# Stage heads of a fused attention and feed-forward kernel: other PSUM banks for the plain tiles, a centring read from PSUM, and another order of the first weight sums

## The chip, the cores and the metric

The kernel runs on one core of one Trainium2 chip. The metric is the device time of one execution in microseconds, taken as the median of several runs. TensorE (PE) multiplies matrices, with PEld for its weight loads; VectorE (DVE), ScalarE (ACT) and GpSimd (POOL) work element by element; SyncE (SP) issues transfers. Each engine takes its instructions in the order in which they were written, and waits for others by semaphores.

## The reference

```python
# q, k, v: (8, 12, 448, 64) float32;  g_ln: (768,);  w_ch1: (768, 3072);  w_ch2: (3072, 768)
scores = matmul(q, k.transpose(0, 1, 3, 2)) / sqrt(64)
attn_out = matmul(maximum(scores, 0.0) ** 2 / 448, v)
x = attn_out.transpose(0, 2, 1, 3).reshape(8, 448, 768)
mu = mean(x, axis=-1);  var = mean((x - mu) ** 2, axis=-1)
xn = (x - mu) / sqrt(var + 1e-06) * g_ln
out = x + maximum(xn @ w_ch1, 0.0) @ w_ch2
```

The division by the root of the variance is one factor per row. Since it is positive it passes through the ReLU, and the kernel multiplies by it at the very end.

## The kernel before, in words

**Stages.** The eight batches go in four pairs. Attention of batches 0 and 1 comes first, interleaved with their first feed-forward layer. Then, for pair 0, 1 and 2, the second layer of the pair (`ffn2`, 56 units of six matmuls: 7 tiles of tokens x 2 halves x 4 parts, L628) is interleaved with the attention of the next pair. Before the second layer of pairs 1 and 2, and of pair 3, stands the first layer of that pair. This place is called a stage head here. There are three: at about 174, 301 and 428 us of the profile.

**Order.** The program order is written out by hand; there is no scheduler that changes it. In `interleave` the attention units are all placed by the last but one of the 56 units, so a stage ends: product of the last attention group (`values`, L363), three units, `centre` of the odd batch, one last unit (L628), whose result DVE finishes with L639.

**Layout.** Activations lie transposed: the 768 channels are six chunks of 128 partitions, and the 448 tokens of a batch lie along the free dimension. `xT` is the attention output, `xc` the same times g_ln, later centred. `lo` and `hi` are the `xc` of the even and odd batch of a pair.

**Centring.** `centre` (L408) sums all channels by matmuls with a matrix of ones (L418) into `sum_ps`. ScalarE copies the sum into SBUF (`total_sb`, L422; only the very first block skips that), and six DVE instructions, one per chunk (L424), subtract the mean from `xc`. For whole batches GpSimd has summed the chunks in advance (L398, L401) and split the sum into two bf16 tiles, `two_sb` (L404, L405).

**PSUM.** There are eight banks. Two belong to `ps_mm` throughout. The other six are, in attention stages, three two-bank tiles of `ps_sc` (scores, products, `sum_ps`), and at the heads of pairs 1 to 3 six one-bank tiles of `ps_m`. A plain tile is one `ffn1` call: six matmuls (L590) into one `ps_mm` bank, then a ReLU on ScalarE (L598) into `hT`. `ffn2` uses `ps_mm` too.

**Heads of pairs 1 and 2.** `ffn1_pair` (L654) computes the first layer for both batches of a pair at once. Of the 24 blocks of hidden channels, four are plain tiles (`beside`: four of the even batch, then four of the odd one). The other twenty go in ten sets of two blocks; in a set the two batches, the two halves of the channels and the two blocks form a 2 x 2 by 2 x 2 product, done with seven block products in place of eight (Strassen). Each product is three matmuls of 448 columns (L715). It needs sums of activations (`x_sum`, and `x[6]` and `x[7]`, L740 and L741, which overwrite parts of `hi` and `lo`), made once a head, and sums of weight blocks, made for each set: two early ones for products 3 and 4 (L694, L695) and three late ones for products 6, 1 and 7 (L702, L706, L707). The order in a set is 3, 4, 1, then 7 and 6 of the set before (`close`), then 5 and 2. DVE adds the results up: L748 and L750 add products 4 and 1 to `z`; L757 and L760 form `z - a` and `z - b`, on which products 7 and 6 are accumulated. Early sums run two sets ahead on GpSimd, late sums one set ahead on DVE.

**Memory of the sums.** `w_room[0]` and `w_room[1]` are attention buffers; `w_room[2]` and the later `z` tiles lie in `room`, the buffer of `xT`, which is free once the transfer L562 has turned `xT` into token order. `temps[0]` and `temps[1]`, the `z` of sets 0 and 1, are the buffers with the tags "total" and "two".

**Head of pair 3.** Here all 24 tiles of each batch are plain tiles, 48 `ffn1` calls. DVE forms weight sums for the second layer meanwhile (L789).

Of the kernel before, what the change touches and what calls it, by code (L numbers as in the profile page):

```python
# [28 lines left out]
def kernel(  # L29
# [22 lines left out]
    nc = tc.nc  # L52
    P = 128
    HP = 64
    bf16 = mybir.dt.bfloat16
    fp32 = mybir.dt.float32

    B, H, S, D = q.shape
# [8 lines left out]
    K2 = d_ff // P  # L67
# [20 lines left out]
    spool = ctx.enter_context(tc.tile_pool(name="stat", bufs=2))  # L88
# [3 lines left out]
    ps_mm = ctx.enter_context(tc.tile_pool(name="ps_mm", bufs=2, space=bass.MemoryType.PSUM))  # L92
# [64 lines left out]
    for queue, name, lo, hi in ((nc.sync, "q", 0, FEW), (nc.scalar, "k", 0, FEW),  # L157
                                (nc.sync, "k", FEW, J), (nc.scalar, "q", FEW, J)):
        s = slice(lo * D, hi * D)
# [139 lines left out]
    FULL = (0, J)  # L299
    FIRST = (0, BLK[0][0])  # L300
# [106 lines left out]

    def centre(b, blk):  # L408
        w = blk[1] * HP
        if (b, blk) == FIRST:  # L410
            ps = ps_mm.tile([P, 512], fp32, tag="mm", name="sum_ps")[:, :w]
        else:
            ps = ps_sc.tile([P, 2, 512], fp32, tag="sc", name="sum_ps")[:, 0, :w]
        rows = [xT[b // 2][:, c, of(blk, b)] for c in range(K1)]
        if blk == FULL:
            rows = [part[b][:, i] for i in range(2)] + (rows[4:] if b % 2 else [])
        for i, r in enumerate(rows):
            nc.tensor.matmul(ps, ones, r, start=(i == 0), stop=(i == len(rows) - 1))  # L418
        total = ps
        if (b, blk) != FIRST:  # L420
            total = spool.tile([P, S], fp32, tag="total", name="total_sb", bufs=1)[:, :w]
            nc.scalar.copy(total, ps)  # L422
        for c in range(K1):
            nc.vector.scalar_tensor_tensor(  # L424
                xc[b][:, c, of(blk)], total, g_mean[:, c:c + 1], xc[b][:, c, of(blk)],
                op0=ALU.mult, op1=ALU.add)
# [152 lines left out]

    since = [9]  # L580

    def ffn1(b, ni, blk):


        pair, o, w = b // 2, b % 2 * S + blk[0] * HP, blk[1] * HP
        if pair not in hT:
            hT[pair] = hpool.tile([P, K2, S2], bf16, tag="hT", name="hT_sb")
        ps = ps_mm.tile([P, 512], fp32, tag="mm", name="h_ps")
        for c in range(K1):
            nc.tensor.matmul(  # L590
                ps[:, :w], w1[:, c, ni * P:(ni + 1) * P], xc[b][:, c, of(blk)],
                start=(c == 0), stop=(c == K1 - 1))
        since[0] += 1
        turns = 2 if (b, blk) == FIRST else 1
        if blk != FULL and since[0] <= turns:
            nc.vector.tensor_scalar_max(hT[pair][:, ni, o:o + w], ps[:, :w], 0.0)
        else:
            nc.scalar.activation(hT[pair][:, ni, o:o + w], ps[:, :w], ACTF.Relu)  # L598
        if since[0] >= turns:
            squares_now()  # L600
# [51 lines left out]
    KQ = K1 // 2  # L652

    def ffn1_pair(pair, rows, beside):  # L654

        lo, hi = xc[2 * pair], xc[2 * pair + 1]  # L660
        hold_x = [apool.tile([P, 2, 512], bf16, tag="attn", name="x_sum")[:, :, :S] for _ in range(5)]
        x = {3: lo[:, :KQ], 4: hi[:, KQ:], 6: hi[:, :KQ], 7: lo[:, KQ:]}
        for m, t, rest in ((5, 0, (3, 0)), (2, 1, (3, 1)), (1, 2, (4, 0))):
            x[m] = (hold_x[t][:, 0], hold_x[t][:, 1], hold_x[rest[0]][:, rest[1]])
        w_room = [[apool.tile([P, 2, 512], bf16, tag="attn", name="w1_sum").rearrange("p r n -> p (r n)")
                   for _ in range(2)] for _ in range(2)]
        temps = [spool.tile([P, S], fp32, tag="total", name="z_sb", bufs=1),
                 spool.tile([P, 2, S], bf16, tag="two", name="z_sb", bufs=1)
                 .rearrange("p i s -> p (i s)").bitcast(fp32)]
        room = xpool.tile([P, K1, S2], bf16, tag="xT", name="room_sb")  # L670
        rest = room[:, KQ:].rearrange("p c s -> p (c s)")
        w_room.append([rest[:, :1024], rest[:, 1024:2048]])
        temps += [room[:, n].bitcast(fp32) for n in range(KQ)]

        def x_sum(m, a, b):
            nc.vector.tensor_add(hold_x[{5: 0, 2: 1, 1: 2}[m]], a[:, :2], b[:, :2])
            (nc.gpsimd if m == 1 else nc.vector).tensor_add(x[m][2], a[:, 2], b[:, 2])

        x_sum(5, lo[:, :KQ], lo[:, KQ:])
        w = {}  # L680

        def blocks(n):
            i, j = rows[n]
            i, j = slice(i * P, (i + 1) * P), slice(j * P, (j + 1) * P)
            return w1[:, :KQ, i], w1[:, :KQ, j], w1[:, KQ:, i], w1[:, KQ:, j]

        def sums_early(n, engine):
            if n >= len(rows):
                return
            b11, b12, b21, b22 = blocks(n)  # L690
            one, two = (t.rearrange("p (c n) -> p c n", n=P) for t in w_room[n % 3])
            w[n] = {2: b11, 5: b22, 6: one[:, :3], 1: one[:, 3:6], 3: two[:, :3], 4: two[:, 3:6],
                    7: (one[:, 6], one[:, 7], two[:, 6]), "61": one[:, :6], "7a": one[:, 6:8]}
            engine.tensor_sub(w[n][3], b12, b22)  # L694
            engine.tensor_sub(w[n][4], b21, b11)  # L695

        def sums_late(n):
            if n >= len(rows):
                return
            b11, b12, b21, b22 = blocks(n)  # L700
            j = slice(rows[n][1] * P, (rows[n][1] + 1) * P)
            nc.vector.tensor_add(  # L702
                w[n]["61"].rearrange("p (h c) n -> p h c n", h=2),
                b11.unsqueeze(1).broadcast_to([P, 2, KQ, P]),
                w1[:, :, j].rearrange("p (h c) n -> p h c n", h=2))
            nc.vector.tensor_add(w[n]["7a"], b21[:, :2], b22[:, :2])  # L706
            nc.vector.tensor_add(w[n][7][2], b21[:, 2], b22[:, 2])  # L707

        def bank():
            return ps_m.tile([P, 512], fp32, tag="m", name="m_ps")[:, :S]  # L710

        def product(n, m, ps, first=True):
            for c in range(KQ):
                at = [a[c] if isinstance(a, (list, tuple)) else a[:, c] for a in (w[n][m], x[m])]
                nc.tensor.matmul(ps, *at, start=(first and c == 0), stop=(c == KQ - 1),  # L715
                                 skip_group_check=not first)

        def relu(n, ps, row, half):
            nc.scalar.activation(  # L719
                hT[pair][:, rows[n][row], half * S:(half + 1) * S], ps, ACTF.Relu)  # L720

        open_ = []

        def close():
            n, a, b = open_.pop()
            product(n, 7, a, False)
            relu(n, a, 0, 0)
            product(n, 6, b, False)
            relu(n, b, 1, 1)

        for unit in beside[:4]:
            unit()
        x_sum(2, hi[:, :KQ], hi[:, KQ:])
        x_sum(1, lo[:, :KQ], hi[:, KQ:])
        sums_early(0, nc.vector)
        sums_late(0)
        sums_early(1, nc.gpsimd)
        for unit in beside[4:]:
            unit()
        nc.vector.tensor_sub(x[7], lo[:, KQ:], hi[:, KQ:])  # L740
        nc.gpsimd.tensor_sub(x[6], hi[:, :KQ], lo[:, :KQ])  # L741
        for n in range(len(rows)):
            z = temps[n] if n < 2 else temps[2 + n % KQ]
            a, b, c = bank(), bank(), bank()
            product(n, 3, a)
            nc.scalar.copy(z, a)
            product(n, 4, b)
            nc.vector.tensor_add(z, z, b)  # L748
            product(n, 1, c)
            nc.vector.tensor_add(z, z, c)  # L750
            if open_:
                close()
            sums_early(n + 2, nc.gpsimd)
            sums_late(n + 1)
            product(n, 5, a, False)
            relu(n, a, 1, 0)
            nc.vector.tensor_sub(a, z, a)  # L757
            product(n, 2, b, False)
            relu(n, b, 0, 1)
            nc.vector.tensor_sub(b, z, b)  # L760
            open_.append((n, a, b))
        return close
# [125 lines left out]

    def ffn1_units(b, blk=FULL):
        if blk == FULL:  # L890
            return [lambda ni=ni: ffn1(b, ni, blk) for ni in range(K2)]
        return [lambda: ffn1_head(b, blk)] + [lambda ni=ni: ffn1(b, ni, blk) for ni in range(3, K2)]

    def ffn2_units(pair):
# [55 lines left out]
    for pair in range(pairs - 1):  # L950
        units = ffn2_units(pair)
        if pair:
            wide.close()
            ps_m = open_narrow()
            tokens(pair)
            first, second = ffn1_units(2 * pair), ffn1_units(2 * pair + 1)
# [18 lines left out]
    ps_m = open_narrow()  # L975
# [56 lines left out]
```

## Time and profile before

| | us |
|---|---|
| runs (median, lowest to highest) | 539.34 (539.16 to 539.63) |
| profiled execution, its own time | 540.06 |
| its span, first to last instruction | 538.3 |
| TensorE busy | 523.7 (97%) |
| DVE busy | 377.7 (70%) |
| ScalarE busy | 281.1 (52%) |
| GpSimd busy | 156.3 (29%) |

The profile shows one execution. A span begins with the first instruction; the execution's own time is 1.76 us longer. A line of the timeline gives start, duration, engine, line, operation, output and inputs, shape and count, and in brackets how long the engine had been idle and which instruction's end released it. Successive instructions of one engine may overlap by a little, so the pitch from start to start is less than the duration. Matmul ends are modelled. The granted TensorE clock is 1.00 of full speed in this profile.

### The profile page before, as it was taken

How to read it: one execution, taken by the hardware profiler on the slowest of the kernel's cores; microseconds unless marked ns; L12 is line 12 of the kernel's file. 1: busy time of each engine (PE TensorE's matmuls, PEld its weight loads, DVE VectorE, ACT ScalarE, POOL GpSimd, SP SyncE). 2: the span in 40 equal slices, each digit the busy share in tenths (PEclk: the TensorE clock that was granted, in tenths of full speed). 3: DMA queues.
4: the chain of work that ended last, by engine and by line, in shares of the span. 5: the costliest groups of instructions: out<-in, count | busy, mean ns of one | idle time of the engine just before them, and what ended most of it. 6: DMA issues, size and time to landing. Idle time of an engine off the chain costs nothing.

```text
span 538.3 us, 11408 instructions
## 1 busy us (share of the span) xinstructions
PE 523.7 (97%) x4666; PEld 309.8 (58%) x4666; DVE 377.7 (70%) x727; ACT 281.1 (52%) x472; POOL 156.3 (29%) x178
## 2 busy tenths in 40 slices
PE   8999999999999999999999989999999999999997
PEld 6677779755555445555555445555555545555665
DVE  5775753378887888767898788757889797024643
ACT  6956775456543366656555256745655244441110
POOL 7334102123425465002625474201230300001321
PEclk9999999999999999999999999999999999999999
DMA  9999999999997901118997950204741150000223
GB/s 198 206 206 207 211 180 179 142 165 155 161 163 135 195 2 13 22 30 137 169 172 149 168 85 2 34 16 84 126 93 44 32 117 1 0 1 2 58 60 88
DMA packets 111301, 56.64 MB, mean 105 GB/s; under 512 B 77330, under 2 KB 111250, under 8 KB 111250
## 3 DMA queue, kind: packets, MB, share of 16 engines
q0 software_dynamic: 26976, 25.50, 31.9%
q1 hardware_dynamic: 83490, 29.77, 30.3%
q8 instruction: 36, 0.59, 0.4%
q10 hardware_dynamic: 784, 0.66, 0.4%
q14 instruction: 15, 0.12, 0.1%
HBM read 51.91 MB, written 11.01 MB: 117 GB/s over the span
## 4 chain that ended last, share of the span: by engine, by line
PE 91%; DMA 2%; DVE 2%; ACT 2%; POOL 2%; issue 1%; DVEq 0%; ACTq 0%; POOLq 0%
PE o_ps L628 31%; PE h_ps L590 23%; PE m_ps L715 12%; PE m_ps L829 8%; PE sc_ps L333 7%; PE av_ps L363 6%; DMA w<-in_moe_w_ch_dram 2%; PE o_ps L884 1%; PE h_ps L612 1%; PE sum_ps L418 1%; ACT hT_sb L598 1%; ACT early L344 1%; PE tr_ps L218 1%; POOL v_sb L128 0%; POOL w L146 0%
## 5 line engine op out<-in xcount | busy, mean ns | idle before, releaser
L628 PE MATMUL o_ps<-w,hT_sb 128*128 128x384 bf16 x1008 | 173.4, 326 | 0.0
L344 ACT ACTIVATE attn_sb<-sc_ps 128x896 bf16<-128x896 f32 (+4 forms) x150 | 126.4, 902 | 82.1 <-PE sc_ps L333 69.3
L628 PEld LDWEIGHTS <-hT_sb 128*128 128x128 bf16 x1008 | 94.9, 98 | 75.0 <-issue 15.2
L590 PE MATMUL h_ps<-xc_sb,w 128*128 128x448 bf16 (+2 forms) x888 | 128.6, 300 | 4.5 <-ACT hT_sb L598 3.8
L590 PEld LDWEIGHTS <-w 128*128 128x128 bf16 x888 | 81.5, 98 | 47.7 <-issue 8.4
L346 DVE TENSOR_TENSOR attn_sb<-attn_sb 128x896 bf16<-128x896 bf16 x126 | 81.6, 662 | 31.6 <-ACT attn_sb L344 29.8
L598 ACT ACTIVATE hT_sb<-h_ps 128x448 bf16<-128x448 f32 (+2 forms) x133 | 59.5, 447 | 64.9 <-PE h_ps L590 64.3
L719 ACT ACTIVATE hT_sb<-m_ps 128x448 bf16<-128x448 f32 x80 | 43.4, 544 | 27.9 <-PE m_ps L715 26.6
L401 POOL TENSOR_TENSOR part_sb<-part_sb,xT_sb 128x448 f32<-128x448 f32 x18 | 23.3, 1295 | 55.1 <-DVE xT_sb L370 54.4
L715 PE MATMUL m_ps<-xc_sb,w_sum 128*128 128x448 bf16 x168 | 36.3, 352 | 2.8 <-DVE m_ps L757 2.8
L424 DVE SCALAR_TENSOR_TENSOR xc_sb<-total_sb,g_mean,xc_sb 128x448 bf16<-128x448 f32 (+2 forms) x54 | 29.0, 606 | 12.8 <-ACT total_sb L422 12.8
L398 POOL TENSOR_TENSOR part_sb<-xT_sb 128x448 f32<-128x448 bf16 x6 | 6.6, 1105 | 105.0 <-DVE xT_sb L370 83.0
L569 DVE BATCH_NORM_STATS2 stats<-xtok_sb 128x6 f32<-128x384 bf16 x56 | 28.0, 541 | 11.3 <-DMA xtok_sb<-xT_sb 11.3
L333 PE MATMUL sc_ps<-qT_sb,kT_sb 64*64 64x448 bf16 x504 | 35.0, 358 | 0.0
L639 DVE SCALAR_TENSOR_TENSOR o_sb<-o_ps,rstd_sb,xtok_sb 128x384 f32<-128x384 f32 (+1 forms) x45 | 26.9, 597 | 9.4 <-PE o_ps L884 5.6
L715 PEld LDWEIGHTS <-w_sum 128*128 128x128 bf16 x210 | 20.4, 98 | 22.5 <-issue 3.6
L370 DVE TENSOR_SCALAR xT_sb<-av_ps 128x896 bf16<-128x896 f32 (+2 forms) x30 | 27.0, 901 | 7.8 <-PE av_ps L363 7.7
L363 PE MATMUL av_ps<-attn_sb,v_sb 64*64 64x448 bf16 (+2 forms) x672 | 32.3, 327 | 0.0
L864 POOL TENSOR_TENSOR z_sb<-z_sb 128x384 f32<-128x384 f32 x3 | 4.2, 1385 | 91.5 <-DVE z_sb L863 82.1
L363 PEld LDWEIGHTS <-v_sb 64*64 64x64 bf16 x840 | 22.7, 107 | 11.8 <-issue 1.6
L386 DVE TENSOR_SCALAR xc_sb<-xT_sb,g_sb 128x448 bf16<-128x448 bf16 (+2 forms) x54 | 26.4, 539 | 1.0
L715 PE MATMUL m_ps<-x_sum,w 128*128 128x448 bf16 x120 | 26.0, 352 | 0.0
(124 smaller groups left out, 584.2 us busy)
## 6 DMA issues: line engine op xcount, KB each, us to landing
out_dram<-o_sb SPq DMA_DIRECT2D x85, 96.0 KB, 2.4
v_sb<-in_v_dram POOLq DMA_DIRECT2D x24, 224.0 KB, 5.4
w<-in_moe_w_ch_dram POOLq DMA_DIRECT2D x12, 384.0 KB, 13.9
w<-in_moe_w_ch_dram POOLq DMA_DIRECT2D x4, 1152.0 KB, 19.9
q_sb<-in_q_dram POOLq DMA_DIRECT2D x20, 224.0 KB, 6.3
k_sb<-in_k_dram POOLq DMA_DIRECT2D x20, 224.0 KB, 5.8
out_dram<-z_sb SPq DMA_DIRECT2D x24, 96.0 KB, 2.2
hold_sb<-in_q_dram POOLq DMA_DIRECT2D x3, 224.0 KB, 11.8
```

The source lines that it names most:

```text
L333: nc.tensor.matmul(ps[cols, r, o * w:(o + 1) * w], g["k"](i)[rows, cols], g["q"](i, r)[rows, blk[0]:sum(blk), cols], start=True, stop=True)
L344: nc.scalar.activation(a, ps[:, :, :len(slots) * w], ACTF.Relu)
L346: nc.vector.tensor_mul(a, a, a)
L363: nc.tensor.matmul(ps[cols, hh, :w], v_sb[rows, pr, j * D:(j + 1) * D], g["attn"][i][rows, r, :], start=(j == 0), stop=(j == J - 1))
L424: nc.vector.scalar_tensor_tensor(xc[b][:, c, of(blk)], total, g_mean[:, c:c + 1], xc[b][:, c, of(blk)], op0=ALU.mult, op1=ALU.add)
L569: nc.vector.bn_stats(stats[:, n], xtok[pair][:, n * G:(n + 1) * G, t, :])
L590: nc.tensor.matmul(ps[:, :w], w1[:, c, ni * P:(ni + 1) * P], xc[b][:, c, of(blk)], start=(c == 0), stop=(c == K1 - 1))
L598: nc.scalar.activation(hT[pair][:, ni, o:o + w], ps[:, :w], ACTF.Relu)
L628: nc.tensor.matmul(ps[:, :DH], hT[pair][:, ki, t * P:(t + 1) * P], w2[:, ki, cols], start=(o == 0), stop=(o == K2 - 1))
L715: nc.tensor.matmul(ps, *at, start=(first and c == 0), stop=(c == KQ - 1), skip_group_check=not first)
L719: nc.scalar.activation(hT[pair][:, rows[n][row], half * S:(half + 1) * S], ps, ACTF.Relu)
L829: nc.tensor.matmul(ps, x[:, ki], y[:, ki], start=(first and ki == 0), stop=(ki == KH - 1), skip_group_check=not first)
```

## The change

The change touches the stage heads only.

- `centre` of a whole odd batch puts its sum into a `ps_mm` bank and DVE reads it there; the ScalarE copy falls away for it. The even batches are as before.
- `ffn1` of a whole even batch uses `ps_m` in place of `ps_mm`: four tiles each at the heads of pairs 1 and 2, all 24 at pair 3.
- In `ffn1_pair` the early sums of set 0 move from DVE to GpSimd, and those of sets 0 and 1 now stand ahead of the activation sums. Set 0's lie in the buffer "two" (`first`), and its third block for product 7 in the first 128 columns of `w_room[0][1]`.
- All activation sums are on DVE: the third part of `x_sum(1)` and `x[6]` come over from GpSimd. `x_sum(5)` now stands behind the first four plain tiles in the program.
- Late sums of set 1 move from the loop's first iteration to the place ahead of the sets. From iteration 1 on, the loop is as before.

```diff
     def centre(b, blk):
         w = blk[1] * HP
-        if (b, blk) == FIRST:
+        straight = (b, blk) == FIRST or blk == FULL and b % 2
+        if straight:
             ps = ps_mm.tile([P, 512], fp32, tag="mm", name="sum_ps")[:, :w]
         else:
             ps = ps_sc.tile([P, 2, 512], fp32, tag="sc", name="sum_ps")[:, 0, :w]
...
-        if (b, blk) != FIRST:
+        if not straight:
             total = spool.tile([P, S], fp32, tag="total", name="total_sb", bufs=1)[:, :w]
             nc.scalar.copy(total, ps)
...
-    def ffn1(b, ni, blk):
+    def ffn1(b, ni, blk, few=False):
...
-        ps = ps_mm.tile([P, 512], fp32, tag="mm", name="h_ps")
+        if few:
+            ps = ps_m.tile([P, 512], fp32, tag="m", name="h_ps")
+        else:
+            ps = ps_mm.tile([P, 512], fp32, tag="mm", name="h_ps")
...
-        temps = [spool.tile([P, S], fp32, tag="total", name="z_sb", bufs=1),
-                 spool.tile([P, 2, S], bf16, tag="two", name="z_sb", bufs=1)
-                 .rearrange("p i s -> p (i s)").bitcast(fp32)]
+        first = spool.tile([P, 2, S], bf16, tag="two", name="w1_sum", bufs=1)
+        first = first.rearrange("p i s -> p (i s)")
+        temps = [spool.tile([P, S], fp32, tag="total", name="z_sb", bufs=1), first.bitcast(fp32)]
...
         def x_sum(m, a, b):
             nc.vector.tensor_add(hold_x[{5: 0, 2: 1, 1: 2}[m]], a[:, :2], b[:, :2])
-            (nc.gpsimd if m == 1 else nc.vector).tensor_add(x[m][2], a[:, 2], b[:, 2])
-
-        x_sum(5, lo[:, :KQ], lo[:, KQ:])
+            nc.vector.tensor_add(x[m][2], a[:, 2], b[:, 2])
...
-        def sums_early(n, engine):
+        def sums_early(n):
...
             one, two = (t.rearrange("p (c n) -> p c n", n=P) for t in w_room[n % 3])
+            if n == 0:
+                two = first.rearrange("p (c n) -> p c n", n=P)
+                last = one[:, 6], one[:, 7], w_room[0][1][:, :P]
+            else:
+                last = one[:, 6], one[:, 7], two[:, 6]
             w[n] = {2: b11, 5: b22, 6: one[:, :3], 1: one[:, 3:6], 3: two[:, :3], 4: two[:, 3:6],
-                    7: (one[:, 6], one[:, 7], two[:, 6]), "61": one[:, :6], "7a": one[:, 6:8]}
-            engine.tensor_sub(w[n][3], b12, b22)
-            engine.tensor_sub(w[n][4], b21, b11)
+                    7: last, "61": one[:, :6], "7a": one[:, 6:8]}
+            nc.gpsimd.tensor_sub(w[n][3], b12, b22)
+            nc.gpsimd.tensor_sub(w[n][4], b21, b11)
...
         for unit in beside[:4]:
             unit()
+        sums_early(0)
+        sums_early(1)
+        x_sum(5, lo[:, :KQ], lo[:, KQ:])
         x_sum(2, hi[:, :KQ], hi[:, KQ:])
         x_sum(1, lo[:, :KQ], hi[:, KQ:])
-        sums_early(0, nc.vector)
         sums_late(0)
-        sums_early(1, nc.gpsimd)
+        sums_late(1)
         for unit in beside[4:]:
             unit()
         nc.vector.tensor_sub(x[7], lo[:, KQ:], hi[:, KQ:])
-        nc.gpsimd.tensor_sub(x[6], hi[:, :KQ], lo[:, :KQ])
+        nc.vector.tensor_sub(x[6], hi[:, :KQ], lo[:, :KQ])
...
-            sums_early(n + 2, nc.gpsimd)
-            sums_late(n + 1)
+            sums_early(n + 2)
+            if n:
+                sums_late(n + 1)
...
-            return [lambda ni=ni: ffn1(b, ni, blk) for ni in range(K2)]
+            return [lambda ni=ni: ffn1(b, ni, blk, b % 2 == 0) for ni in range(K2)]
```

## The prediction

> **What bounds the kernel now.** I read the page's busy times, the chain, the waits of TensorE, then busy time by stretch and the timeline of the stage heads.
>
> ```profile
> PE 523.7 (97%) x4666; PEld 309.8 (58%) x4666; DVE 377.7 (70%) x727; ACT 281.1 (52%) x472; POOL 156.3 (29%) x178
> PE 91%; DMA 2%; DVE 2%; ACT 2%; POOL 2%; issue 1%; DVEq 0%; ACTq 0%; POOLq 0%
> ```
>
> TensorE is busy for 523.7 of 538.3 us and is 91% of the chain. No matmul is removed, so at most the other 14.6 us are to be had. The waits say which of them belong to the heads:
>
> ```profile
> PE h_ps L590 <- ACT hT_sb L598: 3.8, 6, 0.6
> PE m_ps L715 <- DVE m_ps L757: 2.8, 3, 1.3
> ```
>
> The columns are us in all, times, longest. Busy time by stretch places them (length, then PE, PEld, DVE, ACT, POOL):
>
> ```profile
> 173.94:185.58 11.64, 10.38 (x56) 5.27 (x54) 10.49 (x18) 4.34 (x8) 3.62 (x4) 1.00 1.24 218
> 185.58:191.62 6.04, 4.70 (x25) 2.35 (x24) 4.50 (x7) 2.70 (x5) 6.04 (x5) 1.00 0.17 39
> 191.62:199.56 7.94, 7.94 (x42) 4.04 (x42) 7.11 (x16) 5.42 (x10) 4.55 (x6) 1.00 0.01 3
> ```
>
> This is the head of pair 1. Its plain tiles lose 11.64 - 10.38 = 1.26 us, the first product set 6.04 - 4.70 = 1.34, the steady loop nothing. In the head of pair 2 the same rows read 11.64 against 10.37 and 10.34 against 8.84: 1.27 and 1.50. In the head of pair 3 (no product sets) 11.52 against 10.26: 1.26. The three heads lose 3.79 + 2.84 = 6.63 us. The granted clock is 1.00 in every stretch.
>
> The timeline of the first head shows both causes:
>
> ```profile
> 174.22 0.53 ACT L422 COPY total_sb<-sum_ps 128x448 f32<-128x448 f32 x1 [6.17 <-PE sum_ps L418]
> 174.78 3.67 DVE L424 SCALAR_TENSOR_TENSOR xc_sb<-total_sb,g_mean,xc_sb 128x448 bf16<-128x448 f32 x6 [2.67 <-ACT total_sb L422]
> 176.84 1.30 PE L590 MATMUL h_ps<-xc_sb,w 128*128 128x448 bf16 x6 [0.63 <-ACT hT_sb L598]
> 178.37 0.61 DVE L639 SCALAR_TENSOR_TENSOR o_sb<-o_ps,rstd_sb,xtok_sb 128x384 f32<-128x384 f32 x1
> ...
> 188.28 0.99 DVE L702 TENSOR_TENSOR w_sum<-w 128x768 bf16<-128x768 bf16 x1
> 188.81 1.23 POOL L695 TENSOR_TENSOR room_sb<-w 128x384 bf16<-128x384 bf16 x1
> 189.19 0.99 DVE L706 TENSOR_TENSOR w_sum<-w 128x256 bf16<-128x256 bf16 x1
> 190.11 0.93 DVE L707 TENSOR_TENSOR w_sum<-w 128x128 bf16<-128x128 bf16 x1
> 190.96 0.61 DVE L757 TENSOR_TENSOR m_ps<-z_sb,m_ps 128x448 f32<-128x448 f32 x1
> 191.62 1.29 PE L715 MATMUL m_ps<-xc_sb,w_sum 128*128 128x448 bf16 x6 [1.34 <-DVE m_ps L757]
> ```
>
> First, one of the two ps_mm banks holds the last output tile until L639 ends at 178.98, because L639 stands behind six centrings; the plain tiles share the other bank and wait twice for its ReLU. Second, set 1's late sums (L702, L706, L707) take 0.99, 0.99 and 0.93 beside GpSimd, where their medians are 0.55, 0.28 and 0.22; L757 behind them is late, and product 7 waits.
>
> **Even plain tiles in ps_m.** Four tiles of six matmuls follow the last output tile, from 174.91 at 6 x 0.189 = 1.135 us each: they end at 179.45 with no bank shared. The banks were ps_sc's, whose last reader, L370, is done at 171.46 now that the odd sum is in ps_mm: no wait. Gain 0.63 x 2 a head if the odd tiles are ready by 179.45. In pair 3 all 24 even tiles change pools; after the first two waits they ran without a gap, so the term is the same 1.26.
>
> **Odd batch centred from PSUM.** ScalarE's copy (0.53) and a hand-over go: DVE can start at about 174.22 instead of 174.78. Six L424 take 3.67 from SBUF. The trace has the PSUM form only 192 wide, 408 to 418 ns against a minimum of 412 from SBUF: equal, so I keep 3.67 (bound above: L757, which reads and writes PSUM, 0.63 each, 3.8). xc is ready at 177.9, L639 (0.61) ends at 178.45. sum_ps holds the bank whose L639 ended at 169.94, so it does not wait. Both ps_mm banks are free about 1 us before 179.45; that margin is the cover. Without it each microsecond is lost at three heads.
>
> **GpSimd's sets 0 and 1 beside the centring.** Four subtractions, 0.91 us each undisturbed, start once the sum matmuls have released "two" (174.1): done at about 177.9. No path waits for them before 184.3. L639, also a PSUM and an SBUF input, took 0.59 beside GpSimd's L401 (165.19 to 166.67), so I charge the centring nothing; beside a DVE operation of two SBUF inputs GpSimd's took 1.28, so four cost at most 5.1 and end at 179.3, still covered. No DMA moves on GpSimd's queue; its loads were issued by 171.8.
>
> Row for row, the two subtractions of set 0 cost 0.91 each on GpSimd against 0.345 on DVE before: 2 x 0.57 a head if exposed, nothing under the six microseconds of cover that I find. The Trainium skill (GPSIMD Engine Reference, Engine selection) gives VectorE for elementwise work, GpSimd being about twice as slow; by that rule the sum would be rival 3's.
>
> **DVE ahead of the sets.** From 178.45: three pairs of x sums, undisturbed pitch 0.53 + 0.30 each (2.5 us; the first two pairs took 3.66 beside GpSimd before); late sums 0 and 1, 0.81 each by pitch; x7, 0.77: 183.3. x6 must wait until the last odd tile, which it overwrites, has been read. Eight plain tiles from 174.91 without a wait end at 184.0 plus the same pipeline step as before: the sets start at T = 185.58 - 1.26 = 184.32. So x6 runs from about 184.4 to 185.25 (the same length as x7, 0.84, for 2.73 on GpSimd). Behind it in DVE's queue is L748, which came at T + 1.43 before: 185.75, so x6 costs nothing with 0.5 us to spare. Product 1 needs late sums 0 (182.5) at T + 1.1.
>
> **The first set.** L702 to L707 no longer stand ahead of L757. By the rows of before: ReLU at T + 2.47, L757 from T + 3.1 to T + 3.75. Product 7 is due after 15 + 9 matmuls, T + 4.54. The waits of 1.34 and 0.91 go.
>
> **What is late next.** Early sums 2 need xT read by the token transpose. Its landing gave 315.79 in the second head; it follows L639, so T + 3.8 to T + 4.4. Set 0's third block now lies in the columns that early sums 3 write, so GpSimd waits there for product 7 of set 0 (T + 5.2). From then it has six subtractions in a row, to about T + 11. DVE's late sums 2 start at T + 5.55 and meet them: in the second head before they took 2.4 to 2.5 us after L750 (0.71, 0.99, 0.94), by the longest rows 2.9, against 0.81 undisturbed. L757 of set 1 ends at T + 8.5 to T + 9.0, where product 7 of set 1 is due at T + 8.5: 0.05 to 0.5 us in each head, in place of 0 and 0.59. I take 0.3: 0.6 in two. After that GpSimd is held again to one set per 3.97 us.
>
> **Sum.** 3.79 + 2.84 - 0.6 = 6.0 us. The profiled execution took 540.06 us, 1.76 more than its span; I expect 538.3 - 6.0 = 532.3 of span, 534.1 of its own time. Against the median, 0.72 lower, this is 539.34 - 6.0 = 533.3. TensorE has no later wait on these engines in the chain that would give it back: from 191.62, 323.03 and 433.32 it runs on, and both DVE and the tail shift with it.
>
> **Rivals.**
>
> 1. *The collision only moves.* Late sums 2 and 3 both meet GpSimd's backlog for their full length, 0.5 + 0.5 a head, and x sums begin beside early sums, at most 0.3: 2.84 is replaced by 2.6 at most, 1.6 likelier. Then 3.79 + 1.24 = 5.0, 534.3; at worst 4.0, 535.3. For it: GpSimd's run of six; against: DVE has 0.47 us to spare per iteration (3.5 busy of 3.97).
>
> 2. *The odd tiles wait.* If GpSimd blocked each centring for 0.91, six last 5.5, L639 ends at 180.3 and TensorE waits 0.9 in two heads: 6.0 - 1.8 = 4.2, 535.1. The undisturbed L639 row speaks against it. The Trainium skill (SBUF — State Buffer, Who interferes with whom) says that VectorE contends when both its inputs are in SBUF, not with one: by that rule too, this rival fails, and the L639 row agrees.
>
> 3. *GpSimd's first sums are exposed.* If they begin so late (after 182.5) that product 3 waits for both, 1.14 a head is lost: 6.0 - 2.3 = 3.7, 535.6. Before, GpSimd's first operation came at 178.54, held by the centring of xc; sets 0 and 1 do not read xc.
>
> 4. *It does not do what it says.* If the even tiles still wait at the change of pools, 3.79 stays: 539.34 - 2.2 = 537.1. Only sum_ps was read late there (174.75), and it moves away.
>
> 5. *Slower: GpSimd's backlog never drains.* Held by the wait on product 7, its sets keep in step with DVE's late sums, and every iteration costs DVE 2.9 instead of 0.81: 5.6 against 3.97, 1.6 us lost. It decides from four iterations in all: 6.0 / 1.6; over three in each head, 6 x 1.6 - 6.0 = 3.6 lost, 543. For it: in the steady loop GpSimd ends at 200.52 and L702 begins at 200.53, no room at all. Against: GpSimd works 1.83 of 3.97 us and waits 2.2 for TensorE each time, so a backlog drains in two or three iterations.
>
> **How the numbers follow.** Forecast 0.66, around 533.3 (532.7 with no residual). Rival 1: 0.12. Rival 2: 0.05. Rival 3: 0.02. Rival 4: 0.05. Rival 5: 0.07. No change by several of these together: 0.03. A measurement of this kernel can tell 0.2% (1.1 us) from no change. The forecast and rivals 1 to 4 are all faster by more, 0.90, less 0.02 for a rival 4 that keeps the second stall too: 0.88; same 0.05, slower 0.07. The range goes from the whole 6.63 with the runs' own spread (0.3) below it, 532.4, up to the bounds of rivals 1 and 2, 535.4.
>
> **What the profile after would show.** Right: no L590 wait on L598 at the heads; the line of L424 from sum_ps at 448 wide starting within 0.2 us of the sum matmuls, 0.6 to 0.7 each; GpSimd's first four subtractions ended before the x sums; x sums at 0.61 and 0.38; L715's wait on L757 down from 2.8 to 0.1 to 1.0, once per head and for set 1; TensorE's busy time unchanged at 523.7 and the span at 532.3. Wrong: a first even tile that waits for a bank, L424 at 0.9 or more, an odd tile waiting for L639 or L424, or waits of L715 in sets 3 and later.

## The result and the profile after

The changed kernel takes 532.77 us (median of four runs, 532.45 to 533.05) against 539.49: a ratio of 0.9876, 95% interval 0.9859 to 0.9893. The profiled execution took 533.05 us with a span of 531.3, 7.0 less than before. Now and then one run of a kernel, of the one before too, takes about 3 us longer than its others, so medians are compared. Outside the heads hardly anything moved: TensorE is busy for 523.6 us (523.7 before), and each stage between two heads lasts 75.38 us in both profiles.

```profile
PE 523.6 (99%) x4666; PEld 310.8 (59%) x4666; DVE 374.2 (70%) x727; ACT 279.2 (53%) x469; POOL 151.0 (28%) x178
PE 95%; ACT 2%; DVE 2%; issue 1%; DMA 1%; DVEq 0%; ACTq 0%
```

Of the waits of TensorE, the one on the plain tiles' ReLU (3.8 us) is gone from the heads, and the one on the subtraction before product 7 (2.8) is this (us in all, times, longest; L768 is L757 of before):

```profile
PE m_ps L723 <- DVE m_ps L768: 0.7, 2, 0.4
```

Busy time by stretch in the first head (length, then PE, PEld, DVE, ACT, POOL): the plain tiles lose nothing of their 10.06 us, the sets 9.03 - 8.67 = 0.36, the loop behind them nothing.

```profile
174.05:184.11 10.06, 10.06 (x56) 5.28 (x55) 9.42 (x21) 3.80 (x7) 3.40 (x4) 1.00 1.17 231
184.11:193.14 9.03, 8.67 (x46) 4.40 (x45) 7.61 (x12) 5.40 (x10) 5.46 (x6) 1.00 0.25 56
193.14:199.00 5.86, 5.86 (x31) 3.02 (x31) 5.62 (x13) 3.79 (x7) 3.72 (x5) 1.00 0.00 0
```

The timeline of that head, with the rows that answer to those of before:

```profile
173.93 0.90 POOL L702 TENSOR_TENSOR w_sum<-w 128x384 bf16<-128x384 bf16 x1 [2.04 <-PE sum_ps L419]
174.25 3.64 DVE L425 SCALAR_TENSOR_TENSOR xc_sb<-sum_ps,g_mean,xc_sb 128x448 bf16<-128x448 f32 x6 [2.02 <-PE sum_ps L419]
175.03 9.24 PE L594 MATMUL h_ps<-xc_sb,w 128*128 128x448 bf16 x48
176.54 0.90 POOL L703 TENSOR_TENSOR w_sum<-w 128x384 bf16<-128x384 bf16 x1
177.81 0.61 DVE L643 SCALAR_TENSOR_TENSOR o_sb<-o_ps,rstd_sb,xtok_sb 128x384 f32<-128x384 f32 x1
...
183.74 0.86 DVE L751 TENSOR_TENSOR xc_sb<-xc_sb 128x1344 bf16<-128x1344 bf16 x1 [0.43 <-PE h_ps L594]
184.11 1.30 PE L723 MATMUL m_ps<-xc_sb,w_sum 128*128 128x448 bf16 x6
...
189.46 0.91 POOL L702 TENSOR_TENSOR w_sum<-w 128x384 bf16<-128x384 bf16 x1 [0.94 <-PE m_ps L723]
189.62 1.17 DVE L710 TENSOR_TENSOR room_sb<-w 128x768 bf16<-128x768 bf16 x1
190.71 0.99 DVE L714 TENSOR_TENSOR room_sb<-w 128x256 bf16<-128x256 bf16 x1
191.62 0.93 DVE L715 TENSOR_TENSOR room_sb<-w 128x128 bf16<-128x128 bf16 x1
192.47 0.61 DVE L768 TENSOR_TENSOR m_ps<-w_sum,m_ps 128x448 f32<-128x448 f32 x1
193.14 1.29 PE L723 MATMUL m_ps<-xc_sb,w_sum 128*128 128x448 bf16 x6 [0.36 <-DVE m_ps L768]
```

Eight plain tiles run as one stretch of 48 matmuls. GpSimd's four subtractions take 0.90 each beside the centring, which is not held up. What is left is set 1's wait: late sums 2 meet GpSimd, whose early sums 3 were let go at 189.46 by product 7 of set 0.

### The profile page after: what moved, and what is told of

It reads as the page before. It is cut to its first block, busy times and chain, and to the rows that moved or that the text cites. A ratio compares the mean times of both kernels' runs of the same rounds, so it can differ in the third digit from the quotient of the medians.

```text
span 531.3 us, 11402 instructions
## 1 busy us (share of the span) xinstructions
PE 523.6 (99%) x4666; PEld 310.8 (59%) x4666; DVE 374.2 (70%) x727; ACT 279.2 (53%) x469; POOL 151.0 (28%) x178
## 4 chain that ended last, share of the span: by engine, by line
PE 95%; ACT 2%; DVE 2%; issue 1%; DMA 1%; DVEq 0%; ACTq 0%
PE o_ps L632 32%; PE h_ps L594 23%; PE m_ps L723 13%; PE m_ps L840 8%; PE sc_ps L333 7%; PE av_ps L363 6%; PE h_ps L616 2%; PE o_ps L895 1%; ACT early L344 1%; PE tr_ps L218 1%; PE sum_ps L419 1%; DMA stage_sb<-in_q_dram 1%; DVE room_sb L714 0%; PE busy_ps L308 0%; DVE w_sum L758 0%
## 5 line engine op out<-in xcount | busy, mean ns | idle before, releaser
L643 DVE SCALAR_TENSOR_TENSOR o_sb<-o_ps,rstd_sb,xtok_sb 128x384 f32<-128x384 f32 (+1 forms) x45 | 26.8, 597 | 9.6 <-PE o_ps L895 5.6
L840 PEld LDWEIGHTS <-h_sum 128*128 128x128 bf16 x180 | 17.6, 98 | 11.6
```

The source lines that it names most:

```text
L840: nc.tensor.matmul(ps, x[:, ki], y[:, ki], start=(first and ki == 0), stop=(ki == KH - 1), skip_group_check=not first)
```

## The experiments

Two theories are told apart throughout. A: a wait of TensorE costs its idle time in the profile plus some 0.16 us (worked out in the next section), and the changes work only together. B, the rival in most places: the idle time is all, and each part is worth its own waits.

**The banks alone.** The kernel before, with only the first two items of the change:

```diff
+        straight = (b, blk) == FIRST or blk == FULL and b % 2
...
+        ps = (ps_m.tile([P, 512], fp32, tag="m", name="h_ps") if few else
+              ps_mm.tile([P, 512], fp32, tag="mm", name="h_ps"))
```

> Only the two bank changes: even plain tiles in ps_m, odd batch centred from ps_mm; every sum stays where it was before. Theory A (a wait of TensorE costs its idle time in the profile plus about 0.16 us, because the next matmul starts on an empty pipeline: start to start the two waits of a head cost 1.93 - 1.135 = 0.795 each): 6 x 0.795 = 4.8 us less than before, 534.7, with the waits of product 7 on the subtractions still there (1.3 in the first head, 0.5 to 1.5 in the second). Theory B (a wait costs what the profile shows as idle, and the other 1.1 us of the change come from elsewhere): 3.8 us less, 535.7.

Measured: 536.21 us, ratio 0.9940 (0.9917 to 0.9963), span 534.6. The bank waits are gone, but the other wait grew:

```profile
PE m_ps L717 <- DVE m_ps L759: 3.7, 4, 1.3
```

It was 2.8 in three. With the sets starting earlier, both heads now lose 1.27 in set 0 and 0.59 in set 1, where I had expected 1.3 in all in the first head and at most 1.5 in the second. In part by these waits the time is 1.5 us above A's figure, and B's 535.7 is nearer to it; by the time alone this run does not favour A. The profiles do: idle time in the heads fell by 6.64 - 3.73 = 2.91 us and the span by 3.7. B has no place for the other 0.8; by A five waits fewer give it (5 x 0.163).

**The order alone.** The other half: the new order of the sums, with the old banks and ScalarE's copy.

```diff
-        straight = (b, blk) == FIRST or blk == FULL and b % 2
+        straight = (b, blk) == FIRST
...
-            return [lambda ni=ni: ffn1(b, ni, blk, b % 2 == 0) for ni in range(K2)]
+            return [lambda ni=ni: ffn1(b, ni, blk) for ni in range(K2)]
```

> The other half of the change: the new order and engines of the sums, with the even plain tiles in ps_mm and the odd batch centred through ScalarE's copy, as before. Theory A: the centrings (two SBUF inputs) take turns with GpSimd and end at 180.6, the last output's L639 at 181.1, so the even tiles have one bank for longer: three waits of 0.63 in place of two in the heads of pairs 1 and 2, two in that of pair 3, and the wait of set 1: 3 x 0.8 x 2 + 2 x 0.8 + 1.05 = 7.5 us of losses against 8.1 before, 538.8, no real gain from the order by itself. Rival (the order is worth its 2.84 us of product waits by itself): 537.

Measured: 539.75 us, ratio 1.0003 (0.9987 to 1.0020): no change, though the waits on the subtractions are all but gone.

```profile
PE h_ps L594 <- ACT hT_sb L602: 3.8, 6, 0.6
PE h_ps L594 <- DVE o_sb L643: 1.8, 2, 0.9
PE m_ps L723 <- DVE m_ps L768: 0.4, 1, 0.4
```

The centring, held up by GpSimd (5.59 us for six in the first head), ended later, the last output's bank came free later, and in the heads of pairs 1 and 2 a third bank wait (now on L643) took the place. By the ratios banks alone gained 0.6%, order alone nothing, both 1.24%.

**The copy kept.** The changed kernel with `straight = (b, blk) == FIRST` only, so that the centring reads SBUF.

> The changed kernel, but the odd batch is centred through ScalarE's copy in SBUF as before. Theory A: each centring then has two SBUF inputs and takes turns with GpSimd's four subtractions, so six last 5.5 to 6 us in place of 3.64, the subtractions take 1.2 and more, the first odd tile waits 1.3 to 1.9 us in the heads of pairs 1 and 2 and not in that of pair 3, where GpSimd has nothing to do: 535.5 to 537. Rival (the input does not matter, only the 0.6 us of the copy): the centring ends at 178.5, before the odd tiles at 179.57, and the time is that of the changed kernel, 532.8.

Measured: 535.87 us, ratio 0.9939 (0.9918 to 0.9960), span 533.9, some 2.6 more than the changed kernel.

```profile
174.99 5.59 DVE L425 SCALAR_TENSOR_TENSOR xc_sb<-total_sb,g_mean,xc_sb 128x448 bf16<-128x448 f32 x6 [2.67 <-ACT total_sb L423]
175.77 1.29 POOL L702 TENSOR_TENSOR w_sum<-w 128x384 bf16<-128x384 bf16 x1
177.02 1.29 POOL L703 TENSOR_TENSOR w_sum<-w 128x384 bf16<-128x384 bf16 x1
181.16 3.56 PE L594 MATMUL h_ps<-xc_sb,w 128*128 128x448 bf16 x18 [0.18 <-DVE o_sb L643]
```

Six centrings take 5.59 in place of 3.64, and the two of GpSimd's subtractions that lie wholly beside them 1.29 in place of 0.90. At the head of pair 3 of this same kernel, where GpSimd has nothing to do, the same six from SBUF take 3.66. So it is neither the copy nor SBUF by itself, but two SBUF inputs beside GpSimd. The price was right, its place only in part: the odd tiles waited a mere 0.18, as the second of them waited for the bank of L643; the first had a free bank and takes the chunks in the order in which they are centred; the delayed DVE was then late for the first set (0.35 on L758) and for product 7. By the Trainium skill (SBUF — State Buffer, Who interferes with whom) a VectorE instruction with two SBUF inputs contends with a GpSimd instruction that reads SBUF; this run agrees.

**Even tiles back in ps_mm**, the sum still there (`ffn1(b, ni, blk)` without the last argument).

> The changed kernel, but the even plain tiles go back into ps_mm, while the odd sum stays there too. Theory A: the sum holds one bank until the last centring (177.9 in the first head), the last output tile holds the other until 178.4, so the first plain tile waits from 175.03 to 177.95, 2.9 us plus the refill, at three heads: 9 us more than the changed kernel, 541.8, slower than before. Rival: only the sharing of one bank comes back (4.8 us), 537.6.

Measured: 545.15 us, ratio 1.0105 (1.0076 to 1.0133). Slower than before, as expected, by a gap at each head:

```profile
177.69 10.93 PE L594 MATMUL h_ps<-xc_sb,w 128*128 128x448 bf16 x48 [2.76 <-DVE xc_sb L425]
```

But 3.4 us more than expected, and the same 48 matmuls take 10.93 us here where they took 9.24. Busy time by stretch shows why (length, engines' busy time, then the granted clock):

```profile
177.69:180.00 2.31, 2.31 (x10) 1.08 (x10) 2.31 (x6) 0.54 (x1) 0.00 (x0) 0.74 1.25 203
180.00:182.00 2.00, 2.00 (x7) 0.87 (x6) 2.00 (x7) 0.54 (x1) 0.00 (x0) 0.50 1.16 320
182.00:184.00 2.00, 2.00 (x12) 0.98 (x10) 0.28 (x2) 0.54 (x1) 0.00 (x0) 0.94 1.25 282
```

The gap was long enough to halve the clock for 3.41 us, in the first head and the third, not in the second. Three more profiles of the same kernel looked into this.

> The kernel whose even plain tiles wait for the sum's bank, once more, for the granted clock. In its first profile TensorE was idle for 2.76 us at each of the three heads, and the clock was 0.50 for 3.41 us after the first and the third, not after the second. Theory A (the clock goes by the idle share of stretches of 3.41 us that run on regardless of the kernel; over about 2 us idle in one of them halves the next): the drops are 3.41 us long again, come or not by how each gap falls on the grid that the drops show, and each costs 1.7 us: 541.8 with none, 543.5 with one, 545.2 with two, 546.9 with three. Rival (the clock goes by the length of the gap alone, and the second head differed by accident of that run): the same heads drop or all three, with no relation to a grid.

> The kernel with the 2.76 us gaps a third time: in the two profiles so far the clock's changes fell on nearly the same grid (15.23 and 15.22 us after the record began), so they could not tell grid from gap. Theory A: with another grid the stretch of 3.41 us that holds over 2.0 us of a gap, or about that, halves the next, whichever head it is; a gap split near its middle (1.0 and 1.7 in the second head so far) costs nothing. Rival: the first and third head drop and the second does not, whatever the grid.

> As the run before it, once more, for a further grid: by theory A the heads that drop follow from the grid; by the rival they are the first and the third.

They took 545.22, 546.33 and 546.81 us, against 545.2 forecast for two drops and 546.9 for three. The first had nearly the grid of the profile above and the same two drops; the other two had other grids and three drops each. In all four, every change of the clock lies on a multiple of 3413 ns from the first one. The gap of 2.76 us between the modelled end of one matmul and the next is cut by that grid, or lies within one stretch of it; the larger piece was 2.04, 2.16, 2.30, 2.46 and 2.65 to 2.76 us (six times) in the ten heads with a drop, and 1.74 and 1.91 in the two without. So it goes by the idle share of a stretch of the grid, and in these runs the line lies between 1.91 and 2.04 of 3.41 us. That the same heads always drop is refuted by the second head, and that the length of the gap alone decides by its being the same in all twelve. Three drops give spans of 544.5 and 545.0, two give 543.2 and 543.4: 1.4 us apart, near the 1.7 of half a stretch. The Trainium skill (TensorE: Matmul & The Clock Gate, Why this matters for your kernels) asks for no idle gap above about 3 us; its free-running window of 3413 ns (What's actually happening) agrees with the grid, but here gaps of 2.76 did it.

**Late sums 1 back in the loop.**

```diff
         sums_late(0)
-        sums_late(1)
...
-            if n:
-                sums_late(n + 1)
+            sums_late(n + 1)
```

> The changed kernel, but the late sums of set 1 go back into the loop's first iteration. Theory A: they meet early sums 2 on GpSimd in the first head (from T + 2.63), take 2.9 us, and product 7 of set 0 waits 1.3 to 1.6; the wait of set 1 is then gone there; in the second head the token transfer lands only at T + 3.55, after them, and nothing changes: 533.8 (533.3 to 534.5). Rival (the old wait came from x[6] on GpSimd, which is gone): 532.8, no new wait.

Measured: 534.32 us, ratio 0.9908 (0.9884 to 0.9932), span 532.6.

```profile
187.11 1.00 DVE L714 TENSOR_TENSOR w_sum<-w 128x256 bf16<-128x256 bf16 x1
187.93 0.95 POOL L703 TENSOR_TENSOR room_sb<-w 128x384 bf16<-128x384 bf16 x1
188.03 0.93 DVE L715 TENSOR_TENSOR w_sum<-w 128x128 bf16<-128x128 bf16 x1
189.55 1.29 PE L723 MATMUL m_ps<-xc_sb,w_sum 128*128 128x448 bf16 x6 [0.88 <-DVE m_ps L766]
```

The wait of set 0 is back with x[6] on DVE, so the place of these sums makes most of it. It is 0.88, less than forecast, since L710 slipped in 0.02 us before GpSimd and took 0.55. With the banks alone, where GpSimd was at x[6] until 187.31, the same sum took 0.95 and the wait was 1.27: x[6] on GpSimd can account for the other 0.4. The wait of set 1 stayed (0.42) where I had it gone.

**x[6] on GpSimd** (`nc.gpsimd.tensor_sub(x[6], ...)`) and **early sums 0 on DVE** (`engine = nc.gpsimd if n else nc.vector`), beside the changed kernel and the next one:

> The changed kernel itself, beside the three that follow, for comparison on one chip. Both theories: 532.8.

> The changed kernel, but x[6] goes back to GpSimd (2.73 us from T). Theory A: it lies beside additions that read PSUM, which GpSimd does not hold up, ends when the token transfer lands, and product 6 wants it at T + 5.1: no change, 532.8 within 0.3. Rival: GpSimd's early sums 2 and 3 come later by it and collide longer with DVE's late sums 2: 0.5 to 1 us more, 533.5.

> The changed kernel, but the early sums of set 0 go back to DVE, ahead of its activation sums (0.69 us by pitch). Theory A: DVE's work ahead of the sets ends at 183.9 in place of 183.2 and x[6] waits for TensorE until 183.7 anyway: no change, 532.8 within 0.3; that these sums are on GpSimd is worth nothing. Rival (DVE is the limit of the head, so the move was what helped): 0.7 us more in each of two heads, 534.2.

Measured: 533.22 (ratio 0.9869, 0.9841 to 0.9898), 532.87 (0.9863, 0.9836 to 0.9889) and 533.02 (0.9874, 0.9844 to 0.9905). The three cannot be told apart. Neither of these two moves, taken back by itself, costs anything that these runs can show: with late sums 1 out of the loop, where x[6] is done is immaterial, and so is the engine of set 0's early sums.

**The late sums split.** Only L711 stands ahead of the two subtractions; the sums for product 7 follow them, for n from 1 on:

```diff
             if n:
-                sums_late(n + 1)
+                sums_late(n + 1, (0,))
...
             nc.vector.tensor_sub(b, z, b)
+            if n:
+                sums_late(n + 1, (1,))
```

> The changed kernel, but in the loop only the first late sum (for products 6 and 1) stands ahead of the two subtractions on DVE; the other two, which are needed one set later, stand behind them. Theory A: the subtraction of set 1 ends 1.7 us sooner, the one wait left in each head (0.36 us idle, 0.52 start to start) goes: 1.05 us less than the changed kernel, 531.7. Rival (the collision only moves on to the next additions of DVE): a wait of about the same size in set 2, 532.8.

Measured: 531.93 us, ratio 0.9853 (0.9822 to 0.9883), span 530.1. Five of the six runs lie at 531.62 to 532.06, all below the changed kernel's 532.79 to 533.70 on the same chip, and the sixth took 535.04: 1.3 us by the medians.

```profile
189.55 1.17 DVE L711 TENSOR_TENSOR room_sb<-w 128x768 bf16<-128x768 bf16 x1
191.06 0.63 DVE L770 TENSOR_TENSOR m_ps<-w_sum,m_ps 128x448 f32<-128x448 f32 x1 [0.34 <-ACT hT_sb L729]
192.43 0.93 DVE L717 TENSOR_TENSOR room_sb<-w 128x128 bf16<-128x128 bf16 x1
192.55 1.30 PE L725 MATMUL m_ps<-xc_sb,w_sum 128*128 128x448 bf16 x6
```

The collision is still there (L717 takes 0.93), behind the subtraction instead of ahead of it, and TensorE no longer waits in the heads. This is the fastest version of the study.

## Why the prediction was right

The forecast was 533.3 us (532.4 to 535.4); 532.77 came out.

- *Plain tiles.* As forecast: no wait at the change of pools, odd tiles ready in time (L643 ended at 178.42 of a forecast 178.45).
- *Centring.* 3.64 against 3.67, started at 174.25 against 174.22. The SBUF form beside GpSimd loses 2.6 us in all (the copy kept); rival 2, which has each centring blocked in the same way, had priced that at 1.8.
- *DVE ahead of the sets.* x[7] ended at 183.31, forecast 183.3; x[6] ran at 183.74 to 184.60, and L758 at T + 1.40 did not notice.
- *What is late next.* Late sums 2 were it, 0.36 in each head; I had taken 0.3 from 0.05 to 0.5. Its parts, counted from the first matmul T of the sets: the token transfer landed by T + 2.63 and T + 3.56 (forecast for the second head T + 3.8 to T + 4.4), and GpSimd was held until T + 5.35 (forecast T + 5.2).
- *The mis-sized term* is the price of a wait. I took idle time from the profile, 3.79 + 2.84 - 0.6 = 6.0, and measured heads lost 6.64 - 0.72 = 5.92 of it. The span fell by 7.0. The profile models a matmul's end at 0.352 us after its start, while undisturbed matmuls start every 0.189; so a wait that the profile shows as 0.63 is 1.93 - 1.135 = 0.80 from start to start, 0.163 more. For this reason the sets began 10.06 us after the start of the last output unit (at 184.11), not 10.38 (my 184.32). Seven waits fewer are 1.14 us, and 5.92 + 1.14 = 7.06.
- *Luck.* With that term the sum gives 532.2, below the low end of my range (532.4), which took the 6.63 us of idle time for all there was to gain. That 532.77 lies inside the range is in part luck: by the medians the fall is 6.7 and not 7.0, because the profiled execution of before lies 0.57 above its median and that of after 0.28 above. Why, the runs do not show.

The runs bear the price of a wait out. Taking idle time in the heads from the span leaves between 530.1 and 531.7 us, a spread of 1.5; with 0.163 for each wait as well, between 530.1 and 530.3. Three kernels that are not in the table, the changed one again, x[6] on GpSimd and early sums 0 on DVE, come to 529.9 to 530.3; those with the halved clock are left out. What spread remains lies outside the heads. The three heads by themselves, each from the first matmul of the last L628 unit before it to the first one of the pair's own second layer, came down from 160.82 to 153.78 us, by 7.04; less idle time and 0.163 per wait they are 152.72 to 152.76 in all ten kernels. So nothing but TensorE's waits makes the difference between their heads.

| kernel | span | idle in heads, waits | span - idle | - 0.163 per wait | the three heads |
|---|---|---|---|---|---|
| before | 538.29 | 6.64, 9 | 531.65 | 530.19 | 160.82 |
| order alone | 537.45 | 5.91, 9 | 531.54 | 530.07 | 160.09 |
| banks alone | 534.57 | 3.73, 4 | 530.84 | 530.19 | 157.12 |
| copy kept | 533.90 | 2.45, 7 | 531.45 | 530.31 | 156.35 |
| late sums 1 in the loop | 532.60 | 1.89, 4 | 530.71 | 530.06 | 155.27 |
| after | 531.27 | 0.72, 2 | 530.55 | 530.22 | 153.78 |
| split | 530.13 | 0.00, 0 | 530.13 | 530.13 | 152.74 |

Of rival 1 only the meeting with late sums 2 came; late sums 3 took 0.71, 0.28 and 0.21 us in the first head, and nothing waited for them. Of the others, the exposed GpSimd sums, the wait at the change of pools and the backlog that never drains did not come: from 196.29 GpSimd waits for TensorE again.

## What to carry to other kernels

Price a wait of a pipelined engine from start to start, against the undisturbed pitch; the idle time beside it was too small by 0.163 us for each wait here, what a matmul's modelled end has over the pitch, and many short waits make that count. Before freeing an engine, follow each buffer one step on: here banks without order gained half, order without banks nothing, and plain tiles left in the banks that the sum had moved to made the kernel slower than before. When a collision between two engines cannot be avoided, put work that nobody waits for soon into it.

## What the runs showed of the hardware that I had not expected

The granted clock fell to 0.50 for 3.41 us after a gap of only 2.76 us, whenever 2.04 us or more of it lay in one stretch of a 3413 ns grid that does not start with the kernel; where the larger piece was 1.91 us or less, the clock stayed at 1.00. Against the same head of the changed kernel the gap then cost 2.9 us without a drop and 4.2 to 4.6 with one, by chance of the grid.
